# One order table for another in a single-core attention and mixture-of-adapters kernel

## The chip, the core and the metric

The kernel runs on one core of a Trainium2 chip. The metric is device time in microseconds (us) from one launch; less is better. Five engines work side by side, each through its own queue in order: PE (TensorE, matrix products), DVE (VectorE) and ACT (ScalarE), which both read what PE leaves in the PSUM banks, POOL (GpSimd), which here issues the loads, and SP (SyncE), which issues most stores and the transposing DMAs. They meet only through semaphores.

## The reference

```python
scores = scale * np.matmul(q, k.transpose(0, 1, 3, 2))      # 8 batches, 12 heads, 448 x 448, head size 64
attn = np.maximum(scores, 0.0) ** 2 / S
x = np.matmul(attn, v)                                      # heads side by side: 3584 rows of 768
logits = x @ w_gate                                         # 8 experts; the best two get softmax weights w
delta[mask] += w[mask, k, None] * (z @ B[e])                # z = x[mask] @ A[e], rank 16
return (x + delta).astype(np.float32)
```

## The kernel before, in words

`build` makes a list of operations, each with its engine or engines, its PSUM banks and a function that emits its instructions. A long string, `ORDER`, then says in which order they are emitted and so how each engine's queue runs. A word such as `relu148:A` or `qk149@4` names an operation, the engine where two could do it (A for ACT, D for DVE) and the first of its PSUM banks. Nothing is decided at run time: an engine that waits holds up everything behind it in its own queue.

The 24 pairs (batch b, quad q of four heads) go one after another. For a pair, three loads bring q, k and v (kind `load`, words `f..`, issued by POOL, two DMAs each). `tp` turns q and k on PE, `te` copies them out on DVE. Then come seven key blocks: `qk` (scores, PE), `relu` (scale and relu out of PSUM, on ACT, a few on DVE), `sq` (square in place on DVE, two or three blocks at a time) and `pv` (product with v, PE). `x` copies the sums into `xt`, on ACT or DVE. Batch 7 is cut into 322 and 126 columns, so that blocks 147 to 173 are narrower.

Every 128 rows of `xt` are a tile, 28 in all. In groups of three, `z` multiplies with the gate and A weights (PE), `gmax`, `gd`, `gu`, `gt`, `gsg`, `gw`, `gzp` choose two experts and weight z (DVE, `gsg` on ACT), `zt` and `zT` turn it. Each half tile then has a `b` (PE: z with B, on top of x) and an `o` (copy to the output buffer `osb`, four of them). For tiles 15 to 23 the x part comes not from PE but from transposing DMAs on SP (`xb`) and is added by `o` on DVE. `st` stores a tile, mostly from SP.

PE works with 64x64 tiles in `tp`, `qk` and `pv` and with the whole 128x128 array in `z`, `zt` and `b`.

The lines that bind the order are these:

```python
    for word in ORDER.split():
        word, _, b = word.partition("@")
        name, _, e = word.partition(":")
        o = by.pop(name)
        o.eng = next(x for x in o.engs if x.startswith(e))
        if o.want:
            o.banks = [int(b) + i for i in range(o.want[1])]
```

Of the kernel before, what the change touches and what calls it, by code (L numbers as in the profile page):

```python
# [14 lines left out]
J = 7  # L15
CUT = 3
SPIN = 8
PH = 64
QUADS = 3
NB = 8  # L20
S = J * PH
# [12 lines left out]
C = dict(late=6, xi=(), om=(), merge_x=0, sqp=((999, (2, 2, 3)),), om2=(), fl=(), gf=(), ai=4, tg=((15, 3), (18, 3), (21, 3)), sp=(), xbdur=1.45, bx=8, xh=2, apart=3, apcap=1, gl=(3, 1), tqlat=2.0)  # L34
# [5 lines left out]
f4 f3 f1 f0 f2 f6 f5 f8 f7 f11 f9 f10 f84@0 f12 f88 f85@2 f90 f89 f13 f87@4 qk0@6 f91 qk1@0 relu0:D qk2@2 f14  # L40
relu1:A qk3@4 relu2:D relu3:A tp2@6 f17 qk4@0 te2 relu4:A qk5@2 qk6@4 sq2 tp3@6 f16 relu5:A f86@0 te3 relu6:A
sq0 qk7@0 f15 qk8@2 qk9@6 relu7:A tp4@4 relu8:D relu9:A f18 qk10@0 te4 qk11@2 relu10:A qk12@6 sq4 tp5@4 f19
relu11:A qk13@0 relu12:A te5 tp6@2 f26 sq9 relu13:A qk14@4 qk15@6 tp7 relu14:A f23 sq7 pv0@0 pv1 pv2 relu15:A
pv3 qk16@4 te6 pv4 pv5 f20 relu16:A pv6 qk17@6 x13:D pv7@2 relu17:A qk18@4 sq11 f22 pv8 pv9 x12:A qk19@6
relu18:A pv10 qk20@0 relu19:D f21 pv11 relu20:A pv12 pv13 qk21@4 sq16 x27:A qk22@6 f27 qk23@0 relu21:A aw1@3
sq14 relu22:A f33 x26:D relu23:A qk24@4 tp8@6 ae1 f25 relu24:A sq18 qk25@0 qk26@2 tp9 relu25:A f55 pv14@4 pv15
pv16 te8 relu26:A pv17 qk27@0 f31 pv18 pv19 relu27:A pv20 sq23 qk28@2 qk29@6 x41:A f28 qk30@0 x40:D relu28:A
aw0@5 sq25 relu29:A f29 relu30:A qk31@2 ae0 tp10@6 tp11 f32 relu31:A sq21 qk32@4 qk33@0 relu32:A te10 pv21@2 f30
pv22 pv23 relu33:A qk34@4 sq30 qk35@6 relu34:A qk36@0 f37 relu35:D relu36:A qk37@4 pv24 pv25 relu37:A pv26 sq32
f35 qk38@6 tp12@0 pv27 relu38:A tp13 qk39@4 f43 x55:A te12 qk40@6 x54:A z0@3 relu39:A sq35 qk41@0 f34 z1  # L50
relu40:A qk42@4 relu41:D z2 relu42:A f38 qk43@6 gmax0 tp14@0 relu43:A sq28 qk44@4 tp15 f42 relu44:A gd0 qk45@6
# [33 lines left out]
relu137:A sq135 o29:A qk138@0 qk139@6 o26:A qk140@4 st28 relu138:A z15@2 relu139:D z16 xb108 z17 relu140:A
qk141@0 gmax15 pv126@6 pv127 relu141:A gd15 pv128 gu15 qk142@4 gt15 sq133 xb111 pv129 pv130 gsg15 pv131
relu142:A qk143@0 pv132 gw15 b27@3 gzp15 x264:A xb95 x265:D relu143:A zt15@2 zt16 zt17 sq137 pv133@4 o27:A
qk144@6 tp44@0 zT15:A pv134 st26 tp45 relu144:A qk145@2 pv135 te44 pv136 xb109 relu145:A pv137 qk146@6 pv138
pv139 sq140 relu146:A z18@0 xb112 b30@1 x279:A sq142 z19 x278:A qk147@2 qk148@6 o30 qk149@4 xb110 relu147:A z20
sq144 b32@1 relu148:A relu149:A b33@2 gmax18 qk150@6 o32 qk151@4 relu150:A b31@3 gu18 o33 relu151:A gd18 qk152@6  # L90
sq149 st32 b34@1 relu152:A gt18 o31 gsg18 qk153@4 qk154@6 gw18 o34 relu153:A st30 b35@2 gzp18 relu154:A xb113
qk155@4 o35 pv140@0 relu155:A pv141 sq151 qk156@6 pv142 pv143 relu156:A qk157@2 qk158@4 xb126 pv144 pv145
relu157:D relu158:A pv146 tp46@6 tp47 x293:A x292:D qk159@4 qk160@2 xb129 relu159:A zt18@1 te46 zt19 zt20 z21@0
relu160:A z22 sq156 zT18:A qk161@4 qk162@6 xb127 qk163@2 relu161:A b40@1 sq147 relu162:A z23 sq158 relu163:A
xb130 qk164@4 pv147@6 pv148 relu164:A pv149 pv150 o40 qk165@2 pv151 pv152 relu165:A pv153 sq154 qk166@4 st34
b41@1 relu166:A gmax21 xb128 x307:A gu21 qk167@2 gd21 sq163 pv154@4 x306:A pv155 pv156 relu167:A pv157 pv158
qk168@6 gt21 o41 pv159 gsg21 pv160 gw21 b36@2 st40 x320:A gzp21 x321:A sq161 b38@3 relu168:A xb131 zt21@1 sq165
zt22 zt23 qk169@4 zT21:A pv161@6 pv162 pv163 relu169:A pv164 o38 qk170@0 pv165 pv166 o36 relu170:A pv167 b37@3
# [46 lines left out]
def build(k=None, c=C):  # L145
# [31 lines left out]
    def load(b, w, q, deps):  # L177
        nm = "qkv"[w]

        def fn():  # L180
# [7 lines left out]
        o = op(("POOL",), 1.17, fn, deps=deps, kind="load", take=(nm, "lane"), give=("lane",))  # L188
        o.mb = 1.35
        return o  # L190

# [763 lines left out]
```

## Time and profile before

| what | value |
|---|---|
| median of 3 runs | 181.4 us |
| lowest and highest run | 180.84 and 181.58 us |
| profiled execution, span | 179.6 us |
| PE, DVE, ACT, POOL busy | 92%, 91%, 87%, 50% of the span |
| granted clock of TensorE over the span | 1.00 |

The span runs from the first to the last instruction of the profiled execution. That execution's own device time is not listed by itself; the median of the timed runs lies 1.8 us above its span, and times are formed here as span plus 1.8. Busy time is the union of instruction durations. On ACT and DVE consecutive instructions overlap in this record, so a busy share near 100% can still hold short waits.

### The profile page before, as it was taken

What the parts mean: (1) busy time and instruction counts of PE and PEld (TensorE: products, weight loads), DVE (VectorE), ACT (ScalarE), POOL (GpSimd) and SP (SyncE); (2) the same over time, 40 slices, a digit from 0 to 9 for tenths busy, and PEclk for the clock granted to TensorE, in tenths of its full rate; (3) what the DMA queues carried; (4) which work ended last, traced back from release to release, by engine and by line L of the source; (5) the groups of instructions that cost most, each with busy time, mean ns of one, the idle gap of its engine ahead of it and who ended that gap; (6) DMA issues with size and microseconds to landing.
All of it is one profiled execution on the core that took longest, in us unless ns stands there. A gap on an engine that the chain in (4) does not pass through costs nothing.

```text
span 179.6 us, 7694 instructions
## 1 busy us (share of the span) xinstructions
PE 165.1 (92%) x3366; PEld 99.2 (55%) x3366; DVE 163.5 (91%) x254; ACT 156.2 (87%) x240; POOL 90.7 (50%) x155
## 2 busy tenths in 40 slices
PE   7887998888899999999979899999999999999990
PEld 2445476454535665646646465655666557576650
DVE  0699999999989999999999899999999999999831
ACT  3399999999999999999998999999999899993120
POOL 7999997988869377850966867250000000000000
PEclk9999999999999999999999999999999999999999
DMA  4999999999999999994699999988495663515644
GB/s 90 126 170 188 164 112 183 164 180 178 202 180 152 186 303 166 175 166 130 84 176 299 197 185 268 237 118 222 113 171 149 45 223 63 189 42 211 230 194 158
DMA packets 33985, 30.49 MB, mean 170 GB/s; under 512 B 11488, under 2 KB 30432, under 8 KB 33952
## 3 DMA queue, kind: packets, MB, share of 16 engines
q0 software_dynamic: 22000, 17.03, 65.7%
q1 hardware_dynamic: 11376, 11.90, 22.1%
q10 hardware_dynamic: 576, 1.08, 1.6%
q8 instruction: 26, 0.43, 0.9%
q14 instruction: 7, 0.06, 0.1%
HBM read 33.84 MB, written 11.01 MB: 250 GB/s over the span
## 4 chain that ended last, share of the span: by engine, by line
PE 44%; ACT 16%; DMA 16%; POOL 15%; issue 4%; DVE 2%; ACTq 0%; POOLq 0%
PE ps L737 17%; ACT a L472 14%; DMA q<-in_q_dram 9%; PE ps L452 9%; PE ps L520 8%; POOL k L185 5%; PE ps L582 4%; POOL v L185 4%; DMA B<-in_moe_B_dram 4%; POOL q L185 3%; PE ps L728 3%; DMA k<-in_k_dram 3%; PE ps L313 2%; ACT osb L773 2%; PE ps L644 1%
## 5 line engine op out<-in xcount | busy, mean ns | idle before, releaser
L472 ACT ACTIVATE a<-ps 128x896 bf16<-128x896 f32 (+3 forms) x158 | 132.7, 961 | 3.3 <-PE ps L452 3.0
L489 DVE TENSOR_TENSOR a<-a 128x1792 bf16<-128x1792 bf16 (+4 forms) x75 | 88.5, 1193 | 0.0
L452 PE MATMUL ps<-qT 64*64 64x448 bf16 (+2 forms) x756 | 57.9, 345 | 4.5 <-ACT a L472 3.3
L737 PE MATMUL ps<-B,zT 128*128 128x384 f32 x112 | 47.5, 514 | 0.3 <-DMA B<-in_moe_B_dram 0.3
L520 PE MATMUL ps<-a,v 64*64 64x448 bf16 (+2 forms) x756 | 44.3, 330 | 0.8 <-ACT a L472 0.4
L452 PEld LDWEIGHTS <-qT 64*64 64x64 bf16 x756 | 25.3, 106 | 31.9 <-issue 22.9
L185 POOL DMA_DIRECT2D k<-in_k_dram x46 | 27.8, 629 | 16.3 <-PE ps L452 7.1
L185 POOL DMA_DIRECT2D v<-in_v_dram x48 | 28.8, 621 | 8.1 <-PE ps L452 3.8
L185 POOL DMA_DIRECT2D q<-in_q_dram x48 | 29.4, 639 | 3.5 <-DMA v<-in_v_dram 1.5
L520 PEld LDWEIGHTS <-v 64*64 64x64 bf16 x756 | 22.6, 106 | 7.9 <-issue 2.7
L327 DVE COPY qT<-ps 128x1792 bf16<-128x1792 bf16 x21 | 22.8, 1084 | 0.7 <-ACT a L472 0.4
L565 ACT CAST xt<-ps 128x448 bf16<-128x448 f32 (+2 forms) x37 | 19.4, 560 | 2.6 <-PE ps L520 2.3
L773 ACT COPY osb<-ps 128x384 f32<-128x384 f32 x26 | 13.1, 529 | 7.4 <-PE ps L737 5.6
L737 PEld LDWEIGHTS ps<-B,zT 128*128 128x128 f32 x112 | 17.3, 190 | 3.7 <-DMA B<-in_moe_B_dram 0.4
L474 DVE TENSOR_SCALAR a<-ps 128x896 bf16<-128x896 f32 (+1 forms) x16 | 16.9, 1069 | 0.9 <-PE ps L452 0.9
L313 PEld LDWEIGHTS <-q 64*64 64x64 bf16 x672 | 10.4, 112 | 6.9 <-issue 3.3
L582 PEld LDWEIGHTS <-xt 128*128 128x128 bf16 x168 | 10.5, 98 | 5.7 <-issue 4.7
L582 PE MATMUL ps<-awg,xt 128*128 128x136 bf16 x168 | 13.5, 223 | 0.0
L728 PEld LDWEIGHTS <-xt 128*128 128x128 bf16 x114 | 8.0, 98 | 9.9 <-issue 8.1
L313 PE MATMUL ps<-identb,q 64*64 64x64 bf16 x672 | 10.9, 197 | 2.3 <-DMA q<-in_q_dram 1.1
L728 PE MATMUL ps<-identb,xt 128*128 128x128 bf16 x114 | 12.7, 220 | 0.2
L565 DVE CAST xt<-ps 128x448 bf16<-128x448 f32 (+2 forms) x17 | 9.6, 570 | 0.2 <-PE ps L520 0.2
(47 smaller groups left out, 97.9 us busy)
## 6 DMA issues: line engine op xcount, KB each, us to landing
out_dram<-osb SPq DMA_DIRECT2D x25, 384.0 KB, 4.2
q<-in_q_dram POOLq DMA_DIRECT2D x48, 112.0 KB, 5.0
v<-in_v_dram POOLq DMA_DIRECT2D x48, 112.0 KB, 4.9
k<-in_k_dram POOLq DMA_DIRECT2D x46, 112.0 KB, 4.9
out_dram<-osb ACTq DMA_DIRECT2D x2, 384.0 KB, 2.3
B<-in_moe_B_dram POOLq DMA_DIRECT2D x1, 384.0 KB, 6.6
xb<-xt SPq DMA_TRANSPOSE x18, 3.2
a_raw<-in_moe_A_dram POOLq DMA_DIRECT2D x1, 192.0 KB, 5.4
```

The source lines that it names most:

```text
L185: nc.gpsimd.dma_start(out=t[g * PH : g * PH + PH], in_=k.qkv[w][b, g, :, 2 * q : 2 * q + 2, :])
L313: nc.tensor.transpose(k.ps_b[sl * PH : sl * PH + PH, o.banks[g], (w * J + j) * PH : (w * J + j) * PH + PH], source(w, j)[r, sl], k.identb[ ...
L327: nc.vector.tensor_copy(t.rearrange("p g w x -> p g (w x)"), k.ps_b[:, m.banks[0] : m.banks[0] + 2, : 2 * S])
L452: nc.tensor.matmul(out=bank(o, sl)[g * PH : g * PH + PH, at : at + w].rearrange("k (j p) -> k j p", j=J), lhsT=t[r, g, 1, j * PH : j * PH ...
L472: nc.scalar.activation(out, flat(qk_ops[n], w), ACTF.Relu, scale=k.relu_scale)
L474: nc.vector.tensor_scalar(out, flat(qk_ops[n], w), k.relu_scale, 0.0, op0=ALU.mult, op1=ALU.max)
L489: nc.vector.tensor_mul(a, a, a)
L520: nc.tensor.matmul(out=bank(head, g)[sl * PH : sl * PH + PH, :w], lhsT=vn[r, sl, j * PH : j * PH + PH], rhs=T["a", g0][r, x + sl * width(n ...
L565: evac(w, lambda cp, g=g: cp(k.xt[:, g * QUADS + q, b * S + x0 : b * S + x1].rearrange("d (p j) -> d p j", j=J), bank(src, g)[:, :w].rearr ...
L582: nc.tensor.matmul(out=bank(zops[0])[:, t * ZW : t * ZW + ZW], lhsT=k.xt[:, do, 128 * tiles[t] : 128 * tiles[t] + 128], rhs=k.awg[:, do, : ...
L728: nc.tensor.matmul(out=out(h)[:, x * 128 : x * 128 + 128], lhsT=k.xt[:, 3 * h + x, c0 : c0 + 128], rhs=k.identb, start=(x == 0), stop=Fals ...
L737: nc.tensor.matmul(out=o, lhsT=T["zT", g0][:, zi], rhs=rhs, start=xb is not None, stop=True, skip_group_check=True,)
```

## The change

The string `ORDER` is replaced by another one over the same 1113 operations. The words say that it was searched near the one in place, in a replay that also follows the granted clock of TensorE. 41 operations that either engine can do change between ACT and DVE, 246 of 308 bank numbers change, and the order changes on every engine. Beside that, options that were not used are taken out of `build`, and the gate columns move: where z had 128 adapter columns and then 8 gate columns, each expert now has its 16 adapter columns and its gate column next to each other. The number and the shapes of instructions stay as they were.

The diff, cut to a few lines of the table and the code that still emits something else:

```diff
-o30 qk149@4 xb110 relu147:A z20 sq144 b32@1 relu148:A relu149:A b33@2 gmax18 qk150@6 o32 qk151@4 relu150:A b31@3 gu18 o33 relu151:A gd18 qk152@6
+pv138 qk147@2 xb91 xb94 xb109 st26 pv139 qk148@0 b32@4 st24 sq140 sq144 relu147:A xb92 relu148:A b30@5 qk149@0 qk150@2
+o30 x278:A x279:A b34@6 xb126 relu149:A o32 z18@7 o34 qk151@0 qk152@4 z19 xb95 relu150:A z20 qk153@2 sq149 sq142
...
-                    for rhs, lo, hi in ((k.a_raw[:, :, i, :], 0, RE), (k.g_raw[:, i, :], RE, ZW)):
+                    for rhs, lo, hi in ((k.a_raw[:, :, i, :], 0, R), (k.g_raw[:, i, :, None], R, R + 1)):
                         nc.tensor.matmul(
-                            out=bank(m)[:, x * ZW + lo : x * ZW + hi],
+                            out=bank(m)[:, x * ZW : x * ZW + ZW].rearrange("p (e s) -> p e s", e=E)[:, :, lo:hi],
...
-                nc.vector.max(mx[:, t, :], z3()[:, t, RE:ZW])
+                nc.vector.max(mx[:, t, :], zv()[:, t // m, t % m, :, R])
...
+                zv().rearrange("p a t e s -> p a (t e) s")[:, :, :, :R],
```

Counted from the two tables, the operations on each engine (before, then now):

| engine | operation | up to relu90 | then up to relu173 | after it |
|---|---|---|---|---|
| ACT | relu | 81, 82 | 77, 79 | 0, 0 |
| ACT | x | 12, 10 | 21, 23 | 4, 5 |
| ACT | o | 8, 8 | 15, 14 | 3, 5 |
| ACT | zT | 2, 1 | 3, 4 | 1, 1 |
| DVE | relu | 10, 9 | 6, 4 | 0, 0 |
| DVE | sq | 35, 34 | 39, 40 | 1, 1 |
| DVE | o | 3, 3 | 15, 19 | 12, 7 |
| DVE | zT | 1, 2 | 2, 1 | 1, 1 |

The relu more on ACT in the first column is relu0. The two of the second column are relu97 and relu157. On PE, from qk90 up to qk173, the new table has 4 pv more (pv66 to pv69) and one b more (b39 and b46 in, b37 out), and one b less after qk173. Changes of PE between its 64x64 and its 128x128 form rise from 99 to 109, from 56 to 62 of them between qk90 and qk173.

Three places of the order follow. On POOL, before, the loads around the one of q for batch 5, quad 1 (`q_1_2315`); `k_2_2257` is k of batch 7, quad 2:

```order
L185 DMA q_2_2114<-in_q_dram 64x2x448 [waits DMASW2_49]
L185 DMA k_2_2257<-in_k_dram 64x2x448 [waits DMASW3_49,PE_49]
L185 DMA k_2_2257<-in_k_dram 64x2x448 [waits DMASW4_49]
L185 DMA v_2_2289<-in_v_dram 64x2x448 [waits DMASW5_49]
L185 DMA v_2_2289<-in_v_dram 64x2x448 [waits DMASW6_49]
L185 DMA q_1_2315<-in_q_dram 64x2x448 [waits DMASW7_49]
L185 DMA q_1_2315<-in_q_dram 64x2x448 [waits DMASW0_49]
```

On POOL, now, the same load is `q_1_2347`:

```order
L184 DMA k_0_2135<-in_k_dram 64x2x448 [waits DMASW7_49,PE_49]
L184 DMA k_0_2135<-in_k_dram 64x2x448 [waits DMASW0_49]
L184 DMA v_2_2138<-in_v_dram 64x2x448 [waits DMASW1_49]
L184 DMA v_2_2138<-in_v_dram 64x2x448 [waits DMASW2_49]
L184 DMA q_1_2347<-in_q_dram 64x2x448 [waits DMASW3_49]
L184 DMA q_1_2347<-in_q_dram 64x2x448 [waits DMASW4_49]
L184 DMA k_2_2463<-in_k_dram 64x2x448 [waits DMASW5_49,PE_49]
```

The load of q now follows k and v of batches 5 and 3, and k of batch 7, quad 2 comes 15 loads later.

On ACT, before, around relu47 to relu52 (L472 is relu, L565 x, L661 zT):

```order
L619 ACTIVATE sg_1212<-t_1191 128x24 [waits DVE_49]
L472 ACTIVATE a_1198<-ps 128x896 [waits PE_49] x2
L565 CAST xt<-ps 128x448 [waits PE_49]
L472 ACTIVATE a_1282<-ps 128x896 [waits PE_49,Activation_49]
L565 CAST xt<-ps 128x448
L661 COPY zT_1329<-ps 128x384 [waits PE_49]
L472 ACTIVATE a_1282<-ps 128x896 [waits PE_49]
```

On ACT, now (L408 is relu, L472 x):

```order
L529 ACTIVATE sg_1197<-t_1181 128x24 [waits DVE_49]
L408 ACTIVATE a_1217<-ps 128x896 [waits PE_49,Activation_49]
L472 CAST xt<-ps 128x448 [waits PE_49]
L408 ACTIVATE a_1217<-ps 128x896 [waits PE_49] x2
L408 ACTIVATE a_1236<-ps 128x896 [waits DVE_49,PE_49,Activation_49]
L408 ACTIVATE a_1236<-ps 128x896 [waits PE_49]
```

One x and the zT have gone from ACT to DVE here.

On SP, before, from the first transposes of tiles 15 to 17 (`xb_3211`; `xb_3463` is of tiles 18 to 20) on:

```order
L677 DMA_TRANSPOSE xb_3211<-xt 128x3x128 x4
L783 DMA out_dram<-osb_3297 128x768
L677 DMA_TRANSPOSE xb_3211<-xt 128x3x128
L783 DMA out_dram<-osb_3305 128x768
L677 DMA_TRANSPOSE xb_3463<-xt 128x3x128 x2
```

On SP, now (`xb_3227` and `xb_3309` are the same two; `osb_3450` is tile 13 and `osb_3284` tile 12):

```order
L577 DMA_TRANSPOSE xb_3227<-xt 128x3x128 x2
L577 DMA_TRANSPOSE xb_3309<-xt 128x3x128
L656 DMA out_dram<-osb_3450 128x768
L656 DMA out_dram<-osb_3284 128x768
L577 DMA_TRANSPOSE xb_3227<-xt 128x3x128
L577 DMA_TRANSPOSE xb_3679<-xt 128x3x128
```

The fifth transpose of tiles 15 to 17 (word `xb92`), which the first half tile `o30` needs, now stands behind the stores of tiles 13 and 12.

## Rows read from the trace of the kernel before

**Rows 1.** Three stretches: length, busy us of PE, PEld, DVE, ACT, POOL; clock; DMA.

```profile
7.83:82.65 74.82, 68.09 (x1618) 40.67 (x1611) 73.76 (x98) 74.37 (x105) 60.24 (x100) 1.00 1.14 177
82.65:162.30 79.65, 78.02 (x1551) 47.71 (x1537) 77.64 (x121) 77.08 (x123) 23.75 (x40) 1.00 0.79 165
162.30:179.60 17.30, 12.96 (x151) 8.11 (x149) 9.88 (x30) 2.68 (x10) 0.00 (x0) 1.00 0.50 191
```

**Rows 2.** Timeline of ACT, two places: start us, length us, line, operation, tiles.

```profile
71.23 0.61 ACT L565 CAST xt<-ps 128x448 bf16<-128x448 f32 x1
71.64 4.26 ACT L472 ACTIVATE a<-ps 128x896 bf16<-128x896 f32 x5
75.63 0.64 ACT L773 COPY osb<-ps 128x384 f32<-128x384 f32 x1
...
135.74 0.64 ACT L773 COPY osb<-ps 128x384 f32<-128x384 f32 x1
136.09 0.66 ACT L661 COPY zT<-ps 128x384 f32<-128x384 f32 x1
136.47 2.73 ACT L472 ACTIVATE a<-ps 128x896 bf16<-128x896 f32 x3
```

**Rows 3.** Timeline of DVE: a relu and the te behind it.

```profile
82.07 1.08 DVE L474 TENSOR_SCALAR a<-ps 128x896 bf16<-128x896 f32 x1
83.07 1.08 DVE L327 COPY qT<-ps 128x1792 bf16<-128x1792 bf16 x1
```

**Rows 4.** ACT's groups from 82.9 to 162.3 us: count, busy us, mean ns, idle.

```profile
L472 ACT ACTIVATE a<-ps 128x896 bf16<-128x896 f32 x52 | 46.1, 966 | 0.6 <-PE ps L452 0.5
L472 ACT ACTIVATE a<-ps 128x644 bf16<-128x644 f32 x20 | 12.8, 709 | 1.0 <-PE ps L452 0.9
L565 ACT CAST xt<-ps 128x448 bf16<-128x448 f32 x16 | 8.8, 601 | 0.0
L773 ACT COPY osb<-ps 128x384 f32<-128x384 f32 x15 | 7.6, 529 | 0.5 <-PE ps L737 0.3
L472 ACT ACTIVATE a<-ps 128x1008 bf16<-128x1008 f32 x3 | 3.0, 1015 | 0.0
L472 ACT ACTIVATE a<-ps 128x756 bf16<-128x756 f32 x3 | 2.4, 805 | 0.2 <-PE ps L452 0.2
L565 ACT CAST xt<-ps 128x322 bf16<-128x322 f32 x5 | 1.9, 436 | 0.1
L661 ACT COPY zT<-ps 128x384 f32<-128x384 f32 x3 | 1.6, 543 | 0.1
```

**Rows 5.** Timeline of ACT around two of its waits.

```profile
93.03 0.96 ACT L472 ACTIVATE a<-ps 128x896 bf16<-128x896 f32 x1
94.51 0.92 ACT L472 ACTIVATE a<-ps 128x896 bf16<-128x896 f32 x1 [0.52 <-PE ps L452]
...
140.28 1.91 ACT L472 ACTIVATE a<-ps 128x644 bf16<-128x644 f32 x3 [0.22 <-PE ps L452]
142.56 1.95 ACT L472 ACTIVATE a<-ps 128x644 bf16<-128x644 f32 x3 [0.38 <-PE ps L452]
```

**Rows 6.** Timeline of PE at that wait, and of POOL before it.

```profile
93.87 0.41 PE L313 MATMUL ps<-identb,q 64*64 64x64 bf16 x26 [0.91 <-DMA q<-in_q_dram]
...
85.61 1.20 POOL L185 DMA_DIRECT2D k<-in_k_dram  x2 [6.06 <-PE ps L452]
```

**Rows 7.** Timeline of PE: b alone between two qk, and four b together.

```profile
143.68 0.91 PE L737 MATMUL ps<-B,zT 128*128 128x384 f32 x2
144.52 0.47 PE L452 MATMUL ps<-qT 64*64 64x322 bf16 x8
...
160.89 2.82 PE L737 MATMUL ps<-B,zT 128*128 128x384 f32 x8
```

**Rows 8.** DMA issues of the page: count, KB each, median us to landing.

```profile
out_dram<-osb SPq DMA_DIRECT2D x25, 384.0 KB, 4.2
...
xb<-xt SPq DMA_TRANSPOSE x18, 3.2
```

More of the change, by code (lines that the diff above doesn't have):

```diff
@@ L31 @@
 PARTS.update({7: ((0, 322, 1, (0, 1, 2)), (322, 448, 4, (0, 1, 2)))})
[L34 removed]
+C = dict(late=6, sq=((999, (2, 2, 3)),), merge_x=(), two=(), groups=(3, 3, 3, 3, 3, 3, 3, 3, 3, 1), ai=4, tg=((15, 3), (18, 3), (21, 3)))
 GROUP = 2688
@@ L85 @@
[L85 to L98, printed above, removed]
-x335:D sq168 x334:A qk171@4 qk172@0 qk173@6 relu171:A z24@2 o37 z25 relu172:A st36 sq170 b46@3 relu173:A b47@4
@@ L186, in fn @@
                                     in_=k.qkv[w][b, g, :, 2 * q : 2 * q + 2, :])
-        o = op(("POOL",), 1.17, fn, deps=deps, kind="load", take=(nm, "lane"), give=("lane",))
+        o = op(("POOL",), 1.17, fn, deps=deps, kind="load", take=((nm, (b, q)),))
         o.mb = 1.35
@@ L287, in build @@
     while n < NS:
-        sqs = next(x for lim, x in c["sqp"] if n < lim)
+        sqs = next(x for lim, x in c["sq"] if n < lim)
         if sqs is not sqs_:
@@ L537, in pv @@
         return o
-    def idle(n, head, after):
-        def fn():
-            for g in range(2):
-                r = slice(g * PH, g * PH + PH)
-                for sl in range(2):
-                    nc.tensor.matmul(
-                        bank(head, g)[sl * PH : sl * PH + PH, :S], lhsT=k.zeros[r, :PH], rhs=k.zeros[r, :S],
-                        start=False, stop=False,
-                    )
-        return op(PE, S / 2400 + 0.01, fn, after=after, mode="64", kind="spin", ni=8, key=("fl", n))
     def xt_copy(n):
@@ L638, in gate @@
+        o_sg = op(ACT, 0.12, f_sig, deps=[o_t], key=("gsg", g0))
+        o_w = op(DVE, 0.1, f_w, deps=[o_sg], key=("gw", g0))
+        o_zp = op(DVE, dve(n * RE), f_zp, deps=[o_w], free=[(zops[0], None)], give=(("w", g0),), key=("gzp", g0))
         zts = []
@@ L698, in outputs @@
         evs, obs, prev = [], {}, None
-        xi = None
-        if tl in c["xi"]:
-            def f_xi():
-                for do in range(DO):
-                    for i in range(2):
-                        r = slice(i * PH, i * PH + PH)
-                        for j in range(2):
-                            nc.tensor.matmul(
-                                out=bank(xi, i)[j * PH : j * PH + PH, do * PH : do * PH + PH],
-                                lhsT=k.xt[r, do, c0 + j * PH : c0 + j * PH + PH], rhs=k.identb[r, r],
-                                start=(do == 0), stop=False, skip_group_check=True,
-                            )
-            xi = op(PE, 0.17, f_xi, mode="64", kind="xi", deps=xdeps[tl], banks=("o", 2), take=("osb",), ni=8 * DO,
-                    key=("xi", tl))
-        merged = xi is not None and tl in c["om"]
-        two = tl in c["om2"]
+        two = tl in c["two"]
         def osb():
@@ L721, in osb, with out @@
             return T["osb", tl]
+        def out(h):
+            return bank(obs[0], h) if two else bank(obs[h])
         for h in range(2):
-            xb = xb_of.get((tl, h)) if xi is None else None
+            xb = xb_of.get((tl, h))
             def f_b(h=h, xb=xb):
-                for x in range(0 if xb or xi else 3):
+                for x in range(0 if xb else 3):
                     nc.tensor.matmul(
```

328 lines of the change are left out of this document (120 added, 208 removed).

## The prediction

> **What bounds the kernel now.** I first cut the span into three stretches by instructions that stand in both tables: the first begins with relu1 at 7.83 us and ends where relu90 starts, at 82.65; the second ends with relu173, the last relu, at 162.30; the third is the rest. Of the first stretch's 74.82 us ACT is busy 74.37 and DVE 73.76; of the second's 79.65 us PE is busy 78.02, DVE 77.64 and ACT 77.08; in the last 17.30 us only PE has much to do, 12.96 [rows 1]. The granted clock is 1.00 in all three, the 2.4 GHz level [rows 1]. So until 162 us no single engine is the limit: two or three are near full and wait for each other in turns. Behind that, PE works off what is left.
>
> Second view: what an instruction really takes from its engine. On ACT five relus start from 71.64 to 75.63, 0.80 apart, though one is recorded as about 1.0 long; from an x to the next start it is 0.41, from an o 0.35, from a zT 0.38 [rows 2]. On DVE a relu takes 1.00 [rows 3]. I count with these steps, not with the recorded lengths.
>
> Third view: how much ACT waits in the second stretch. Its groups there [rows 4] times their steps: 52 relus x 0.80 = 41.6; 20 narrow relus x 0.60 (three of them last 1.91 with a last one of 0.71, so two steps of 0.60 [rows 4, 5]) = 12.0; 16 x of 448 columns x 0.41 = 6.6; 15 o x 0.35 = 5.3; 3 zT x 0.38 = 1.1; scaled by width, 3 relus of 1008 x 0.90 and 3 of 756 x 0.68 = 4.7 and 5 x of 322 x 0.31 = 1.6; five sigmoids, which I put at 0.8 together. That is 73.7 of 79.65 us, so ACT waits 5.9, more than twice the 2.57 us that its busy time leaves open [rows 1].
>
> Fourth view: two of these waits. The relu at 94.51 could have started at 93.03 + 0.80 = 93.83 and is 0.68 late [rows 5]. PE stood still for 0.91 us just before, until 93.87, when a load of q had landed; that load stands on POOL behind one of k that began only at 85.61, since POOL had waited 6.06 us for PE to be done with its buffer [rows 6]. The other: three narrow relus from 140.28 would have let the next start at 142.08; it starts at 142.56 [rows 5], in a place where the old table has z and two b between two qk.
>
> **The change, term by term.** No instruction is added or taken away: work moves between engines, and waits move.
>
> First stretch. Between relu0 and relu90 ACT has 80 relus in both tables, but two x less (0.82) and one zT less (0.38): 1.2 us. DVE gets relu0 and one sq less and a zT more; the sq only comes later, in the second stretch. The relu0 that goes to ACT lies ahead of relu1, in the head, and I take it as free; if relu1 had to start later for it, it would cost up to its 0.80. ACT, the fuller of the two, loses 1.2 and DVE does not gain work, so relu90 comes earlier by **-1.2**. The bound on the other side is 0, if DVE alone set the pace here.
>
> Second stretch. ACT gets two relus more (0.80 and a narrow 0.60), two x more (0.41 and 0.31), a zT more (0.38) and an o less (0.35): **+2.1**. DVE gets two relus less (1.00, and 0.74 by width), the sq from above (1.0, as wide as the te after the relu in [rows 3]), four o's more (0.5 each, by width against the relu with a margin) and a zT less (0.5): about +0.8, hidden beside ACT's 2.1, and if ACT were not the limit it would stand in its place. PE gets four pv more (0.19 each, an estimate from 448 columns at the 2.4 GHz level), one b more and six changes of form.
>
> A b and a change of form: four b's in a row last 2.82 with a last one of 0.91, so three steps of 0.64; a single b between two qk takes from 143.68 to 144.52, 0.84 [rows 7]. Two changes thus cost 0.20, one 0.10. PE's second stretch grows by 0.76 + 0.64 + 0.60 = 2.0.
>
> Against this stands what the new table makes of the 5.9 us of waits. The trace of before can't show that; the bounds are 0 and 5.9. One piece is firm. In the new POOL order the load of q_1 no longer stands behind the k that waited 6.06 us. It landed at about 93.87 [rows 6]; six us earlier is 87.8, and PE wants it at 93.87 - 0.91 = 92.96. That gives the 0.68 back. Of the other 5.2 I take a quarter, 1.3: most of them are for PE, and PE's own work grows in the same stretch, which puts the value nearer to the lower bound. **-2.0**.
>
> Third stretch. In it ACT is busy 2.68 of 17.30 us [rows 1], so PE's list sets the end; the new table leaves one b less behind qk173 (b39 and b46 come earlier, b37 later): **-0.6**. Its cover is that the moved b is counted in PE's 2.0 above and hides beside ACT's 2.1 there; without the cover the gain is 0.
>
> The gate columns: `gmax`, `gu` and `gzp` read as many PSUM elements as before with another step, and `aw` runs twice in all. I take 0; DVE hides it, and if each of the ten groups lost 0.1 us, uncovered, it would be 1.0.
>
> **Sum.** -1.2 + 2.1 - 2.0 - 0.6 = -1.7 us on a span that ends at 179.60 [rows 1]: 177.9. With the 1.8 us by which the median of the timed runs (181.4) lies above the span, this is **179.7 us**.
>
> **A rule against it.** The rows say that a change of form costs PE about 0.10 us [rows 7], and the new table has ten more of them. The Trainium skill, TensorEngine Tiling (Array Packing), section Tiling Modes, says that switching the tiling mode, other than just going to another tile, makes the TensorE drain. By this rule the ten would be a loss of about 1.0 us where PE is the limit throughout; the trace agrees that a change costs time, and gives the price. What they would do here is part of the second rival.
>
> **Rivals.**
> 1. *The forecast*, 179.7; its own range 178.6 to 180.5.
> 2. *PE is the limit behind 82 us, and the waits only move.* For it: PE is busy 78.02 of 79.65 us there [rows 1], and the wait at 142.56 lies behind a block of z and b. Against: it did stand idle 0.91 us at 93 [rows 6]. Then the second stretch grows by PE's 2.0, in place of ACT's 2.1 - 2.0: -1.2 + 2.0 - 0.6 = +0.2, so 181.6.
> 3. *A store on SP holds DVE up, which makes it slower.* The transpose `xb92` now stands behind the store of tile 13, whose last o (o27) now comes after relu144 and an x: in before's times at 136.47 + 0.80 + 0.41 = 137.7, done at about 138.2 with its recorded 0.64. Two store issues of about 0.4 each on, the transpose goes out at 139.0 and lands a median 3.2 later [rows 8], 142.2. DVE gets to `o30` behind sq144, which follows relu146: 139.20 [rows 2] + about 1.5 (2688 columns at 1.0 for 1792 [rows 3]) = 140.7. So DVE stands 1.5 us at the median. It has room for some of that, since it lost work earlier, and ACT feels it only through the banks of qk151 and qk152, which `o32` and `o34` must free; I hold it in what the waits keep. Should the transpose take twice its median, 6.4, DVE stands 4.7, and what passes to ACT is taken as 4.7 less the 1.5 already held: -1.7 + 3.2 = +1.5, 182.9. It decides from a landing of about 5 us on, where the forecast's gain is gone.
> 4. *The table frees more than I allow*, 4 us of the 5.9: -3.7, so 177.7. For it: DVE gets three relus less in all, at 1.00 each [rows 3], and most of what waits for DVE gets shorter. Against: PE's growth.
>
> Through the clock I expect nothing: it is at 1.00 in all three stretches [rows 1], so there is nothing to win, and a stretch at the 1.2 GHz level in the new trace would be a loss that none of these holds.
>
> **Chances.** Forecast 0.48, rival 2 0.26, rival 3 0.14, rival 4 0.12. Half a per cent, 0.9 us, is about what a measurement here tells from no change. Faster than 180.5: most of the forecast (0.43) and rival 4, 0.55. Within: the forecast's upper end (0.05) and most of rival 2 (0.20), 0.25. Slower than 182.3: rival 3 and the upper end of rival 2 (0.06), 0.20. The range goes from just under rival 4 to just under rival 3, 177.5 to 182.8, and leaves out about 2 in 10.
>
> **What would show it.** Right: relu90 starts near 81.5, PE has no wait for q near 92, relu173 ends near 161.2, and about 16.7 us remain behind it. Wrong in the first or second term: relu173 not before 162.3. Rival 2: ACT's waits in the second stretch still near 5.9, with PE full. Rival 3: a wait of DVE before `o30` or `o32` well over 1.5 us, with SP behind the store of tile 13. Wrong also: POOL holding a q again that PE needs.

## The result, and the profile after

The changed kernel takes 183.26 us (median of 9 runs, 182.37 to 185.2), the kernel before 181.4 us beside it (9 runs, 180.84 to 182.28). The ratio is 1.0102, 95% interval 1.0071 to 1.0134. Ratios, here and below, are formed from the fast runs of both kernels alone; a run over 1.5% above the fastest of its kernel counts as slow. The changed kernel is slower by 1% where 1% faster was forecast, and its median lies outside the range. Of the rivals it is the third that the trace shows.

The three stretches of the changed kernel, cut at the same relus as in [rows 1]: length, busy us of PE, PEld, DVE, ACT and POOL, granted clock, DMA share, GB/s.

```profile
7.63:82.75 75.12, 68.41 (x1550) 40.38 (x1550) 72.19 (x97) 73.25 (x104) 61.30 (x102) 0.95 1.14 180
82.75:164.50 81.75, 80.47 (x1600) 47.71 (x1592) 78.12 (x122) 78.61 (x127) 22.55 (x38) 1.00 0.77 155
164.50:181.40 16.90, 12.56 (x152) 7.85 (x149) 7.93 (x26) 3.87 (x13) 0.00 (x0) 1.00 0.55 211
```

Against [rows 1] the first stretch is 0.30 longer, the second 2.10, the third (to the end of the span) 0.40 shorter. Two things are new: the clock of the first stretch, 0.95, and a wait in the second. The wait first. The timeline of DVE, PE, ACT and SP there (start us, length us, operation, tiles, idle before and what ended it):

```profile
138.15 2.55 DVE L425 TENSOR_TENSOR a<-a 128x1792 bf16<-128x1792 bf16 x2
142.29 1.49 DVE L643 TENSOR_TENSOR osb<-ps,xb 128x384 f32<-128x384 f32 x3 [1.60 <-DMA xb<-xt]
...
143.37 0.33 PE L388 MATMUL ps<-qT 64*64 64x322 bf16 x4 [1.26 <-DVE osb L643]
...
143.75 0.71 ACT L408 ACTIVATE a<-ps 128x644 bf16<-128x644 f32 x1 [0.82 <-PE ps L388]
...
136.57 0.81 SPq L656 DMA_DIRECT2D out_dram<-osb  x2
137.43 8.80 SPq L577 DMA_TRANSPOSE xb<-xt  x6
```

Read upward: SP stands at the store of tile 13 until o27 is done, issues it and that of tile 12, then the transpose `xb92`. DVE waits 1.60 us for it before `o30`, PE 1.26 us for the bank that `o32` frees, and ACT 0.82 for that qk. The chain that ended last goes through it (start us, length us, what):

```profile
135.91 0.64 ACT osb L646
...
136.57 0.33 SPq L656
...
136.96 0.43 SPq L656
...
137.43 4.74 DMA xb<-xt
...
142.77 0.56 DVE osb L643
```

The transpose lands 4.74 us after its issue. Now the head. These windows are from 7.8, 10 and 15 us on (columns as above):

```profile
7.80:10.00 2.20, 1.04 (x40) 0.74 (x38) 0.73 (x2) 1.55 (x2) 2.20 (x5) 0.61 1.06 147
10.00:15.00 5.00, 4.86 (x115) 2.38 (x108) 4.86 (x7) 4.77 (x6) 3.89 (x7) 0.50 1.16 170
15.00:20.00 5.00, 3.78 (x113) 2.35 (x113) 5.00 (x5) 4.14 (x6) 4.12 (x7) 0.99 1.09 147
```

PE waits for a load of q, 0.35 and then 0.81 us. The granted clock falls between the two waits, at about 8.3 us by the 0.61 of the first window, and stays at 0.50, the 1.2 GHz level, until 15 us:

```profile
8.19 0.22 PE L312 MATMUL ps<-identb,q 64*64 64x64 bf16 x2 [0.35 <-DMA q<-in_q_dram]
9.22 0.58 PE L312 MATMUL ps<-identb,q 64*64 64x64 bf16 x26 [0.81 <-DMA q<-in_q_dram]
```

### The profile page after: what moved, and what is told of

Read it like the earlier page. It is cut to its first block, busy times and chain, and to the rows that moved or that the text cites. A ratio compares the mean times of both kernels' runs of the same rounds, so it can differ in the third digit from the quotient of the medians.

```text
span 181.4 us, 7687 instructions
## 1 busy us (share of the span) xinstructions
PE 167.0 (92%) x3366; PEld 98.2 (54%) x3366; DVE 160.4 (88%) x249; ACT 158.6 (87%) x245; POOL 90.4 (50%) x155
## 4 chain that ended last, share of the span: by engine, by line
PE 46%; ACT 37%; issue 7%; DMA 5%; POOL 2%; SPq 0%; DVE 0%; DVEq 0%; ACTq 0%; POOLq 0%
ACT a L408 31%; PE ps L619 15%; PE ps L388 11%; PE ps L443 8%; PE ps L490 4%; PE ps L312 4%; ACT osb L646 3%; PE ps L614 3%; DMA xb<-xt 3%; ACT xt L472 2%; DMA q<-in_q_dram 2%; POOL q L184 1%; PE ps L257 1%; PE ps L554 1%; POOL k_rest L215 1%
## 5 line engine op out<-in xcount | busy, mean ns | idle before, releaser
L408 ACT ACTIVATE a<-ps 128x896 bf16<-128x896 f32 (+3 forms) x161 | 136.7, 978 | 5.2 <-PE ps L388 5.1
L388 PE MATMUL ps<-qT 64*64 64x448 bf16 (+2 forms) x756 | 60.4, 346 | 5.5 <-ACT a L408 2.4
L443 PE MATMUL ps<-a,v 64*64 64x448 bf16 (+2 forms) x756 | 43.6, 330 | 0.7 <-ACT a L408 0.6
L388 PEld LDWEIGHTS <-qT 64*64 64x64 bf16 x756 | 24.6, 106 | 33.4 <-issue 26.3
L646 ACT COPY osb<-ps 128x384 f32<-128x384 f32 x27 | 15.1, 590 | 6.7 <-PE ps L619 6.7
L472 ACT CAST xt<-ps 128x448 bf16<-128x448 f32 (+2 forms) x38 | 19.7, 570 | 0.4 <-PE ps L443 0.2
L410 DVE TENSOR_SCALAR a<-ps 128x896 bf16<-128x896 f32 x13 | 14.1, 1085 | 1.2 <-PE ps L388 0.8
L643 DVE TENSOR_TENSOR osb<-ps,xb 128x384 f32<-128x384 f32 x18 | 9.6, 552 | 2.1 <-DMA xb<-xt 1.6
```

What stands on the lines that cost most here:

```text
L388: nc.tensor.matmul(out=bank(o, sl)[g * PH : g * PH + PH, at : at + w].rearrange("k (j p) -> k j p", j=J), lhsT=t[r, g, 1, j * PH : j * PH ...
L408: nc.scalar.activation(out, flat(qk_ops[n], w), ACTF.Relu, scale=k.relu_scale)
L443: nc.tensor.matmul(out=bank(head, g)[sl * PH : sl * PH + PH, :w], lhsT=vn[r, sl, j * PH : j * PH + PH], rhs=T["a", g0][r, x + sl * width(n ...
L472: evac(w, lambda cp, g=g: cp(k.xt[:, g * QUADS + q, b * S + x0 : b * S + x1].rearrange("d (p j) -> d p j", j=J), bank(src, g)[:, :w].rearr ...
L646: cp(osb()[:, h * W : h * W + W], out(h)[:, :W])
```

## The experiments

Times are medians, ratios are to the kernel before on the same chip with 95% interval. "Stretch 2" is from the start of relu90 to the end of relu173 in the profiled execution. Two executions of 375 us (e9_act1, the profiled one) and 853 us (e10_pe1) were disturbed and are left out, of the medians too. e1_sp is the base of most other kernels.

**The transpose, and the code alone.** The table of the changed kernel with one word moved:

```diff
-pv138 qk147@2 xb91 xb94 xb109 st26 pv139 qk148@0 b32@4 st24 sq140 sq144 relu147:A xb92 relu148:A
+pv138 qk147@2 xb91 xb94 xb109 xb92 st26 pv139 qk148@0 b32@4 st24 sq140 sq144 relu147:A relu148:A
```

> The changed table with one word moved: the transpose xb92 goes out on SP ahead of the store of tile 13 and not behind it. Theory S (the wait of DVE for this transpose before o30, 1.60 us in the changed kernel, is passed on to PE and ACT, and stays to the end): no DVE wait for xb between 138 and 145 us, relu160 about 1.3 to 2 us earlier, the end 1.2 to 2.0 us earlier than the changed kernel: 181.2 to 182.0 us, 0.999 to 1.003 of the kernel before. Rival P (PE has no room left there and the wait only moves): DVE's wait is gone, the end moves less than 0.5 us: 182.8 to 183.3, ratio about 1.01.

181.13 us, ratio 0.9989 (0.9959 to 1.0019). That is 0.0113 less than the changed kernel, 2.0 us (0.9 to 3.2 by the ends of both intervals). At relu90 and still at relu146 the two are 0.1 us apart (137.72 and 137.62 at relu146); relu160 comes at 149.29 in place of 150.72. Its timeline of DVE has no such wait, and stretch 2 is 1.47 us shorter:

```profile
138.26 2.55 DVE L428 TENSOR_TENSOR a<-a 128x1792 bf16<-128x1792 bf16 x2
140.73 1.01 DVE L646 TENSOR_TENSOR osb<-ps,xb 128x384 f32<-128x384 f32 x2
```

```profile
7.98:82.86 74.88, 67.71 (x1550) 40.28 (x1550) 72.55 (x97) 73.44 (x103) 60.82 (x101) 0.98 1.14 180
82.86:163.14 80.28, 80.27 (x1600) 47.59 (x1592) 78.04 (x122) 78.46 (x127) 22.55 (x38) 1.00 0.77 157
163.14:180.00 16.86, 12.56 (x152) 7.84 (x149) 8.01 (x26) 3.87 (x13) 0.00 (x0) 1.00 0.55 211
```

Theory S holds. The same wait, put into the kernel before (`xb92` and `xb95` taken out of their places and put behind `st26`):

```diff
-b29@2 sq130 relu136:A xb92 b26@3
+b29@2 sq130 relu136:A b26@3
...
-tp44@0 zT15:A pv134 st26 tp45 relu144:A
+tp44@0 zT15:A pv134 st26 xb92 xb95 tp45 relu144:A
```

> The kernel before, its table as it was but for xb92 and xb95, which now stand right behind the store of tile 13 on SP, as xb92 does in the changed table. In the kernel before that store goes out at 143.3 us, a transpose behind it would land near 146.3, and o30 is wanted near 141.5. Theory S (a wait of DVE for the transpose there goes through to the end): DVE waits 4 to 5 us before o30, and the end is 3 to 5 us later: 184.4 to 186.4 us, ratio 1.017 to 1.027. Rival: the room in front of relu173 takes most of it up, less than 1.5 us: below 182.9.

182.56 us, ratio 1.0052 (1.0011 to 1.0094). The expectation took the wrong store: 143.3 us is when the store of tile 16 goes out; that of tile 13 goes out at 136.4 before and at 135.53 here. So DVE's wait is 1.12 us and not 4 to 5:

```profile
140.38 0.56 DVE L764 TENSOR_TENSOR osb<-ps,xb 128x384 f32<-128x384 f32 x1 [1.12 <-DMA xb<-xt]
```

From relu135 to relu160 it takes 22.63 us, the kernel before 21.46: the 1.12 us come through whole. The time lies below the 182.9 of this expectation's rival, but that bound was set for a wait of 4 to 5 us and tells nothing of one of 1.12. A longer wait of the same kind came by itself in e13_st (below), together with a fall of the clock.

The old table in the new code:

> The table of the kernel before in the changed code: nothing is left of the change but the gate columns and their step in PSUM. As the prediction had it, nothing: 181.0 to 181.8 us, ratio 0.998 to 1.002. Rival: each of ten groups loses 0.1 us on DVE, uncovered: 182.4, ratio 1.0055.

181.19 us, ratio 1.0012 (0.9978 to 1.0045): the code and the gate columns cost nothing. Its profile is a second one of the old order. The clock there is 0.98 in the first stretch (0.66 from 15 to 20 us), and stretch 2 is 1.0 us shorter than in [rows 1]; the wait of 0.91 us for q [rows 6] is not there:

```profile
8.09:83.46 75.37, 68.46 (x1618) 41.06 (x1611) 73.62 (x98) 74.39 (x105) 60.63 (x99) 0.98 1.13 175
83.46:162.10 78.64, 78.05 (x1550) 47.68 (x1537) 77.39 (x121) 76.89 (x123) 23.73 (x40) 1.00 0.80 167
162.10:179.40 17.30, 12.96 (x151) 8.12 (x149) 9.89 (x30) 2.69 (x11) 0.00 (x0) 1.00 0.50 191
```

**The head.** The head of the old table was put on the new one (all words up to te5), once by itself and once with xb92 moved as in e1_sp:

```diff
-f1 f6 f8 f7 f3 f11 f4 f0 f2 f9 f12 f10 f84@0 f5 f85@2 f88 f89 f90 f13 f14 f15 f17 f16 f18 f21 qk0@2 relu0:A f87@0
+f4 f3 f1 f0 f2 f6 f5 f8 f7 f11 f9 f10 f84@0 f12 f88 f85@2 f90 f89 f13 f87@4 qk0@6 f91 qk1@0 relu0:D qk2@2 f14
...
```

> The changed table with the first part (all words up to te5, relu12 among them) in the order, on the engines and in the banks of the kernel before; behind it the changed table as it is. Theory H (in the changed head PE stands and waits for a load of q at 7.8 to 9.2 us, the granted clock falls to half for 6.8 us, and that time is lost): the clock stays at 1.00, relu15 starts near 17.7 and relu30 near 30.2 in place of 32.1, and 1 to 1.8 us of it reach the end: 181.4 to 182.3 us, ratio 1.000 to 1.005. Rival M (the middle has room and makes up for the head in any case): relu30 is earlier, relu90 is not earlier than 82.5, and the time stays at 183.0 to 183.5, ratio 1.01.

> Both of these edits together in the changed table: head of the kernel before, and xb92 ahead of the store of tile 13. If both theories, S and H, hold, their gains add: about 3 us less than the changed kernel, 179.7 to 180.7 us, ratio 0.991 to 0.996, faster than both. If only one holds: 181.2 to 182.3. If PE has no room behind 82 us: about 183.

e2_head 185.09 us, ratio 1.0210 (1.0161 to 1.0258); e3_both 183.22, ratio 1.0114 (1.0064 to 1.0164). Against each other they repeat theory S: 1.9 us less with xb92 forward. For the head they say nothing: at the seam PE now has pv0 ahead of qk14 and waits 1.02 us for v, ACT 1.76 for PE, so that relu13 comes at 16.21 in place of 17.77 but relu15 at 20.05 in place of 19.37. A seam at relu22 (e5_head) was no better: the banks of the two tables overlap there and part of the sums is overwritten.

> The changed table with xb92 ahead of the store of tile 13 (as in e1_sp), and all words up to relu22 in the order, on the engines and in the banks of the kernel before; this seam, other than that of e2_head, has no pv moved ahead of a qk. Theory H (the head of the changed table loses time that reaches the end): relu22 and relu30 1 to 1.7 us earlier than in e1_sp, and 0.8 to 1.7 us at the end: 179.4 to 180.3 us, ratio 0.990 to 0.994. Rival M (what the head loses is given back behind it, since the stretch up to 82 us has waits of its own): relu30 earlier, relu90 less than 0.5 us earlier, 180.7 to 181.5 us, ratio 0.996 to 1.001.

184.72 us, ratio 1.0191 (1.0135 to 1.0247); PE stands 1.67 us before relu30, which comes at 34.82. So theory H was not tested by a graft. What tells more is the same table in several executions. e16_st2 (below) has the words of the changed table up to relu146, but for the order of SP, and its clock stayed at 1.00: its first stretch is 73.89 us. In e1_sp the clock fell at 15 to 20 us, and it took 74.88; in the changed kernel's profile from 8.3 to 15 us, and it took 75.12. The other profiles with this table up to relu90 and no work added there say the same: with no fall in it the stretch takes 73.4 to 74.0 us (seven profiles, e16_st2 among them), with one 74.3 to 75.1 (four, these two among them). Only e15_forms stands apart: 75.44 us at a row of 1.00, but its matmuls of qk last 0.57 us from 9 to 13.5 us, as long as those of the changed kernel at 0.50. In some of these profiles loads came late in the same place, so the difference is not the clock's alone.

**Which engine sets the pace.** e1_sp with work doubled on one engine: a qk or a relu is run twice and writes the same numbers again.

```diff
-            for i, j in enumerate(js):
+            for i, j in list(enumerate(js)) * (1 + (n in MORE_QK)):
...
+            for _ in range(1 + (n in MORE_RELU)):
```

> e1_sp with 20 qk between relu92 and relu135 run twice (80 matmuls more, about 3.8 us of PE at 0.19 a qk; the second run writes the same numbers). Theory P (behind 82 us PE has no room: it is busy 80.27 of the 80.28 us of that stretch in e1_sp): nearly all of it reaches the end, +3.2 to +4.0: 184.3 to 185.1 us. Theory A (ACT sets the pace there, as the prediction's second term has it, and PE has room): +0.5 to +2: 181.6 to 183.1 us.

> e1_sp with five relus of ACT between relu95 and relu130 run twice (5 x 0.80 = 4.0 us of ACT more). Theory P: ACT has 1.8 us of room by its busy time and PE sets the pace, so at most half reaches the end, +0.5 to +2.2: 181.6 to 183.3 us. Theory A (ACT sets the pace): +3.2 to +4.0: 184.3 to 185.1 us.

> e1_sp with four relus of DVE, 99, 107, 122 and 139, run twice (4 x 1.0 = 4.0 us of DVE more). Theory P: DVE has 2.2 us of room by its busy time, +0.5 to +2: 181.6 to 183.1 us. If all three engines are equally the limit there, as little room on any of them: +3 to +4: 184.1 to 185.1 us, and then e6_pe2 and e7_act2 come out as much later.

> e1_sp with five relus of ACT ahead of 82 us, 36, 44, 53, 62 and 72, run twice (5 x 0.80 = 4.0 us of ACT more). Theory A1 (ACT sets the pace of the first stretch, as the prediction's first term has it): relu90 3.2 to 4 us later, the end as much: 184.3 to 185.1 us. Rival (the stretch waits for loads and can hide it): relu90 less than 2 us later, the end at 181.6 to 183 us.

> e1_sp with 20 qk ahead of 82 us, 36 to 45 and 60 to 69, run twice (about 3.8 us of PE more). PE is busy 67.71 of 74.88 us there. Theory A1 (ACT sets the pace, PE has 7 us of room): relu90 less than 1.5 us later: 181.3 to 182.6 us. Theory R (the engines wait for each other in turns there too, and none has room): 3 to 4 us later, 184 to 185 us.

| kernel | added | time | ratio (interval) | stretch 2 (e1_sp 80.28) |
|---|---|---|---|---|
| e6_pe2 | 3.8 us on PE | 186.73 | 1.0308 (1.0235 to 1.0380) | 85.24 |
| e7_act2 | 4.0 us on ACT | 185.99 | 1.0276 (1.0212 to 1.0340) | 84.98 |
| e8_dve2 | 4.0 us on DVE | 185.82 | 1.0257 (1.0194 to 1.0320) | 84.20 |
| e9_act1 | 4.0 us on ACT, first stretch | 185.83 | 1.0247 (1.0160 to 1.0335) | |
| e10_pe1 | 3.8 us on PE, first stretch | 187.07 | 1.0284 (1.0186 to 1.0381) | 80.69 |

In the second stretch the added work comes through whole on any of the three engines: 4.96, 4.70 and 3.92 us more. Neither theory P nor theory A fits all three; R (the engines wait for each other, and none has room) does. For the first stretch the times say the same, but the traces do not settle it. e9_act1 has a profile of the disturbed execution only. The profiled execution of e10_pe1 is the fastest of its three (184.97 us); in it relu90 starts at 84.39, 1.5 us later than in e1_sp, about what theory A1 allows, with the clock at 0.96. How much room PE has there stays open.

Then less work was tried: 88 matmuls of pv between pv72 and pv132, first in e1_sp, then with the stores of e16_st2; and four relus from ACT to DVE, with four sq left out.

```diff
-                for sl in range(2):
+                for sl in range(1 if n in LESS_PV and 0 < j < J - 1 else 2):
```

> e1_sp with 88 of the pv matmuls between pv72 and pv132 left out (about 4.1 us of PE less at 0.19 for a pv of four; these products are missing in the sums, so the output is another). Theory P (PE alone sets the pace behind 82 us): 2.5 to 4 us earlier, 177.1 to 178.6 us. Theory R (PE, ACT and DVE wait for each other in turns, none alone is the limit): less than half of it, 179.3 to 181.1 us.

> e16_st2 with the same 88 pv matmuls between pv72 and pv132 left out as in e11_pe_less (the output is another). In e11_pe_less relu90 to relu135 took 44.34 us, no less than the 43.84 of e1_sp, and what made it slower came behind 155 us. Theory R (PE alone is not what sets the pace behind 82 us): relu90 to relu135 within 0.5 us of e16_st2, and without the late stores the end at 180 to 181.5 us. Theory P (PE alone is): 2.5 to 4 us less, 177.3 to 178.8 us.

> e16_st2 with four relus, 96, 103, 113 and 124, on DVE and not on ACT (3.2 us of ACT less), and four sq of 2688 columns (95, 102, 109, 123) left out to make room on DVE (6 us less, 4 us more; the output is another). Theory A (ACT sets the pace there, and PE only follows): relu90 to relu135 2 to 3.2 us shorter, the end at 178.1 to 179.5 us. Theory P: no gain, 180.7 to 181.5 us. Theory R (each waits for the others): less than 1.2 us.

None gains: e11_pe_less 183.67 (ratio 1.0103, 1.0020 to 1.0186), e17_pe_less2 181.74 (1.0043, 1.0008 to 1.0078), e18_act_less 183.35 (1.0126, 1.0084 to 1.0169). But the edit of pv took no time off PE. It left two of the four matmuls of a pv, and these two last as long as the four. Three pv's in a row with four matmuls each (e16_st2) and with two each (e17_pe_less2):

```profile
119.92 0.76 PE L446 MATMUL ps<-a,v 64*64 64x448 bf16 x12
```

```profile
121.17 0.74 PE L448 MATMUL ps<-a,v 64*64 64x448 bf16 x6
```

So the "4.1 us of PE less" of these expectations were close to none, and e11_pe_less, e14_pe_less_st and e17_pe_less2 say nothing for or against theory P. Stretch 2 of e17_pe_less2 and of e18_act_less:

```profile
81.91:162.41 80.50, 80.30 (x1516) 47.64 (x1508) 78.28 (x122) 78.59 (x127) 22.54 (x38) 1.00 0.79 162
```

```profile
81.67:164.53 82.86, 79.99 (x1604) 47.69 (x1596) 76.54 (x122) 76.63 (x123) 22.57 (x38) 1.00 0.75 156
```

In e18_act_less the four relus on DVE made waits of their own: PE waits 2.9 us for DVE in this stretch, 1.5 of them for one te, where e16_st2 has no wait of PE on its list, and the stretch is 2.6 us longer than the 80.27 of e16_st2. So it does not show what less work on ACT alone is worth. Whether one engine sets the pace behind 82 us is left open by these runs. Both ACT and PE are close to it: ACT is busy 58.00 of the 58.00 us from 82 to 140 in e1_sp, and the list of waits has none of PE in stretch 2 there.

PE's busy time cannot decide it either: with 88 matmuls less it is 80.30 of 80.50 us, as full as before. The Trainium skill, Perfetto Trace Analysis, section Identifying the Most-Contended Engine, takes the engine with the highest occupancy as the one to improve first, and warns that TensorE's busy share does not measure its headroom. The rows agree with the warning: a matmul of pv is recorded with 0.35 us, but three pv's in a row take 0.76, so the records overlap and can fill a stretch that the engine does not fill.

**The stores.** What made e11_pe_less slow stands behind 155 us: DVE waits 2.09 us for the landing of the store of tile 19, whose buffer o36 takes.

```profile
160.55 0.56 DVE L648 TENSOR_TENSOR osb<-ps,xb 128x384 f32<-128x384 f32 x1 [2.09 <-DMA out_dram<-osb]
```

Three late stores were moved forward (tiles 14, 15 and 20), in e13_st with that of tile 15 right behind o31, in e16_st2 behind xb128. The two of tiles 14 and 15, as in e16_st2:

```diff
-qk147@2 xb91 xb94 xb109 xb92 st26 pv139
+qk147@2 xb91 xb94 xb109 xb92 st28 st26 pv139
...
-xb113 xb130 xb128 pv149 gt21 pv150 o40
+xb113 xb130 xb128 st30 pv149 gt21 pv150 o40
```

> e1_sp with three stores moved forward on SP: that of tile 14 ahead of that of tile 13, that of tile 15 right behind o31, that of tile 20 right behind o41. In the changed table the stores of tiles 14 and 15 go out 27 and 16 us after their last o, so that o36 and o46 have to wait for the landings of the stores of tiles 19 and 20 (in e1_sp they start 0.13 and 0.12 us behind these landings). Theory T (these landings hold DVE, and through it PE, at 156 to 166 us): no wait of DVE for a store's landing, the end 0.5 to 1.2 us earlier than e1_sp: 179.9 to 180.6 us, ratio 0.991 to 0.996, faster than both tables. Rival (0.6 us of waits of DVE is all, and PE is full there in any case): 180.8 to 181.4 us, ratio 0.997 to 1.000.

> e13_st with the same 88 pv matmuls left out as in e11_pe_less (the output is another). Theory T: what made e11_pe_less slow was the landing of the store of tile 19, 4.5 us after its issue, which held DVE 2.1 us and PE 1.9 us; with the stores forward it ends no later than e13_st: 179 to 180.6 us. Theory R adds that less PE work alone gives little: not below 178.5. Rival (the end waits for something else): still 182.5 to 184 us.

> e13_st with three places on PE put together: z11 beside z10, zt15 to zt17 beside b27, z19 and z20 beside z18, which takes six changes of form out of the stretch behind 82 us. If PE's changes of form are at the bottom of what the new table lost there: 6 x 0.10 = 0.6 us earlier than e13_st. Theory R (no engine alone is the limit): within 0.4 us of e13_st, or later by the 0.3 us that qk103, qk145 and qk151 each stand further back.

> As e13_st, but the store of tile 15 stands behind the transposes of tiles 18 to 23 (right behind xb128) and no longer ahead of xb127 and xb110, where it held SP until o31 and made DVE wait 4.0 us for xb110. Theory T (the late landings of the stores of tiles 19 and 20 hold o36 and o46): no wait of DVE for a landing behind 150 us, 0.5 to 1.2 us earlier than e1_sp: 179.9 to 180.6 us, ratio 0.991 to 0.996, faster than both tables. Rival (PE is full there in any case and the 0.6 us of waits cost nothing): 180.8 to 181.4 us, ratio 0.997 to 1.000.

e13_st takes 186.5 us, ratio 1.0297 (1.0251 to 1.0344), for the same reason as in theory S. SP stands at the store of tile 15 until o31, 146.04 us, and with it the transposes behind; xb110 lands 4.92 us after its issue, DVE waits 3.95 us for it before o40, PE 3.6. The chain, and DVE:

```profile
149.18 0.42 SPq L659
...
149.65 4.92 DMA xb<-xt
```

```profile
154.75 0.56 DVE L646 TENSOR_TENSOR osb<-ps,xb 128x384 f32<-128x384 f32 x1 [3.95 <-DMA xb<-xt]
```

While PE stands in this stall the clock falls as well (from 150 and from 160 us on, columns as above):

```profile
150.00:160.00 10.00, 6.40 (x54) 3.33 (x53) 4.76 (x14) 4.30 (x10) 0.00 (x0) 0.75 0.49 145
160.00:170.00 10.00, 10.00 (x172) 6.27 (x171) 8.55 (x16) 6.86 (x11) 0.00 (x0) 0.91 0.27 91
```

So the 5 us by which e13_st is slower than e16_st2 (186.5 and 181.3) are the wait and the fall together.

e14_pe_less_st (ratio 1.0269) and e15_forms (1.0239) have the same stall in them and tell nothing on what they were made for. e16_st2 is without it: 181.3 us, ratio 1.0019 (0.9993 to 1.0045). DVE no longer waits for a landing, and o36 and o46 run together at 157.94. Theory T falls by the time, which is in its rival's range. In the trace the last stretch is 0.4 us shorter than that of e1_sp (16.47 against 16.86), but in every run of e16_st2 2.4 to 2.5 us lie between span and time, in those of e1_sp and of the kernel before 2.0 to 2.1; why is not known. Its stretches:

```profile
7.77:81.66 73.89, 67.10 (x1553) 39.07 (x1554) 72.71 (x97) 73.23 (x104) 60.94 (x102) 1.00 1.15 183
81.66:161.93 80.27, 80.26 (x1604) 47.79 (x1596) 78.34 (x122) 78.45 (x127) 22.60 (x38) 1.00 0.79 162
161.93:178.40 16.47, 12.21 (x148) 7.55 (x145) 7.58 (x24) 3.86 (x13) 0.00 (x0) 0.96 0.50 193
```

No kernel here is faster than the kernel before.

## Why the prediction was wrong

**The step that failed: "It has room for some of that ... I hold it in what the waits keep".** The third rival had the place, the cause and, in part by luck, the times right: o30 wanted at 140.7 (140.73 in e1_sp), the transpose landed at 142.2 (142.17), DVE standing 1.5 us (1.60). It then let those 1.5 us vanish in 5.9 us of waits, and priced only what went beyond. Measured, a wait of DVE there comes through whole: 1.12 us gave 1.2 from relu135 to relu160, 1.60 gave 1.5 in stretch 2 and about 2 in the medians. The luck is in the landing: it took 4.74 us where the median of 3.2 [rows 8] was taken, the issue came 1.6 us earlier than reckoned, and the two errors cancelled.

**In the sum it is the -2.0.** By the third view's count ACT has 73.7 + 2.1 = 75.8 us of work in the new second stretch. The +2.1 is in the counts of the table and came in full; what ACT waits besides is 81.75 - 75.8 = 5.95 us in the changed kernel, as much as the 5.9 of before. So nothing of the -2.0 is left. Without the stall (e1_sp) it is 80.28 - 75.8 = 4.5: the new order won 1.4, and the stall took it back.

Even these 1.4 are mostly no merit of the new order. The "firm piece", the q that waits behind k, cost PE 0.91 us in the profile of before, but 0.5 in e12_rev and nothing in e4_code, with the same order of the loads; in e4_code ACT's waits are 78.64 - 73.7 = 4.9. Against that profile the new order wins 0.4, and its second stretch is 1.6 longer. All of the loss is late: from relu90 to relu135 it takes 43.84 us (e1_sp) against 44.00 (e4_code), from there to the end of relu173 36.44 against 34.64. The prediction read ACT's waits as room of which a third could be won; the runs with added work show no such room on ACT, DVE or PE in this stretch. Why the order loses there is not shown.

**The first term, -1.2,** was about right: 73.89 in e16_st2 against 74.82, both at a clock of 1.00, is -0.93; e1_sp against e4_code, both at 0.98, is -0.49. relu90 stands at 81.66 in e16_st2, where near 81.5 was forecast. In the changed kernel the fall of the clock and the late loads hide it: 75.12.

**The third term, -0.6:** from the end of relu173 to that of the last o, 13.55 us before, 13.08 in the changed kernel: -0.47.

**The clock.** "Through the clock I expect nothing" rested on one profile in which it never fell. The timed executions have mean clocks from 0.975 to 1.000 in the changed kernel (9 runs) and likewise from 0.975 to 1.000 in the kernel before (23 runs beside e1_sp), so falls belong to both, and the old profile was a good case. Its 1.00 does not cover all of the stretch either: from 6.8 to 9.8 us its matmuls of qk last 0.56 us on the mean, from 10 to 14 us 0.38. The price by the rows, late loads included: 1.0 us of the first stretch in e1_sp, 1.2 in the changed kernel, against e16_st2. With this the profiled span closes: 1.5 for the transpose, 1.2 for the clock and the loads, 0.6 for the second term, less 0.9 and 0.5, is 1.9; measured 1.8.

**Spans and times.** By these terms the table without the stall should be faster by the 1.2 us by which e16_st2's span (178.4) lies under that of before (179.6). The medians do not show it (1.0019, 0.9993 to 1.0045), and the spans of the timed runs say why: their median is 178.85 us for e16_st2 and 178.8 for the kernel before beside it. The span of the profile of before lies 0.8 us above that median, the one of e16_st2 0.45 below. With the second stretch of e4_code, which has no wait for q, the old order would end at 7.83 + 74.82 + 78.64 + 17.30 = 178.6. The prediction's 1.8 us between span and time has the same fault: single runs of the kernel before lie 2.0 to 2.1 us above their own spans.

**What stays open.** The medians give the stall about 2 us, its trace 1.5. The price of changes of form was not measured apart: the one run for it had the stall of e13_st.

**The gate columns at 0** held (e4_code). Rival 2's sign, ACT's waits still near 5.9 with PE full, is there in the changed kernel (5.95; PE 80.47 of 81.75 us), but e1_sp shows that 1.5 of it is the stall. Whether PE is the limit behind 82 us, as that rival says, was not tested: no run took time off PE.

## What to carry to other kernels

Where stores and loads that somebody waits for share one queue, each store stands for the wait of everything behind it: look for the transfer that has the shortest way to its reader, and put it ahead of the stores whose data come late. Idle time of an engine is not room as long as it waits for its neighbours in turns; run some of its work twice before counting on it. Before a run with less work is read, look whether the engine's time went down with the work: here half the matmuls of a pv took as long as all. A profile is one execution: a wait for a load or a clock that it shows, or does not show, may be otherwise in the next.

## What the runs showed of the hardware

A transpose right behind stores lands late. Issued behind two stores it took 4.7 us, the last four of its row of six in the changed kernel 2.4 (count, median us to landing, from 136.5 and from 141.05 us on):

```profile
out_dram<-osb SPq DMA_DIRECT2D x2, 384.0 KB, 4.6
xb<-xt SPq DMA_TRANSPOSE x1, 4.7
```

```profile
xb<-xt SPq DMA_TRANSPOSE x4, 2.4
```

In the changed kernel the store of tile 12 lands at 141.76 and xb92 at 142.17; in e1_sp the same store at 141.81 and the transpose then behind it (xb126) at 142.27. It is not always 0.4 us: in e13_st the store ahead of xb110 lands at 152.53 and xb110 at 154.56. The Trainium skill, DMA: Bandwidth & Descriptors, section Queues, rings and completion order, says that each DMA engine takes the descriptors of a ring in order, and that a later one may still finish earlier. The trace agrees with the order, these transposes landing 0.4 to 2.0 us behind the store ahead; that one finishes earlier no run here shows.

The clock fell in some executions of a table and not in others, in the same stretch: from 15 to 20 us it is 0.66 in e4_code and 1.00 in the profile of before, with PE busy 3.73 and 3.94 of the 5 us ahead of it. What decides between them was not found.

Two of the four 64x64 matmuls of a pv take as long as all four: 0.74 us for three pv's in a row, against 0.76.
